# A linear-attention block and a token mixer on one core: five whole-operand weight sums move from VectorE to GpSimd

## The chip, the cores and the metric

The kernel runs on one core of a Trainium2 chip. The metric is the device time of one execution in microseconds (us). A core has a matrix engine (TensorE, "PE" in the profile, with its weight loads listed apart as "PEld"), VectorE ("DVE"), ScalarE ("ACT"), GpSimd ("POOL") and SyncE ("SP", which here only issues DMAs). Each engine works through its own queue in order, and they wait for one another by semaphores.

## The reference

The block has two halves with a residual each: linear attention with 32 heads over 2048 tokens of width 1024, then a mixer that multiplies along the token axis with a hidden width of 3584.

```python
def _B_ref(x, w1, b1, w2, b2):
    h = _layernorm(x, axis=-1)
    u = jnp.einsum("bsd,sf->bdf", h, w1) + b1
    u = _gelu(u)
    y = jnp.einsum("bdf,fs->bds", u, w2) + b2
    return (lambda x, *d: x.transpose(*d))(y, 0, 2, 1)

x = A_x
h = x + _A_ref(_layernorm(x, axis=-1), A_wqkv, A_wo)
h2 = h + _B_ref(_layernorm(h, axis=-1), B_w1, B_b1, B_w2, B_b2)
return h2
```

The change is in the first product of `_B_ref`, h (2048 x 1024, contracted over its 2048 tokens) with w1 (2048 x 3584).

## The kernel before

**Two levels of seven products.** Each of the mixer's two matrix products is made by a Strassen-Winograd scheme: a 2 x 2 block product from seven block products in place of eight, at the price of sums of operands beforehand and of results afterwards. The outer level splits tokens and columns in halves; for five of its seven products (1, 2, 3, 5 and 6) an inner level does the same again. Products 4 and 7 are made plainly.

**Names.** w1 is loaded in seven pieces, one for each `Quad` (a "pair of pairs": two `Mixer1`, each a pair of hidden blocks of 128). In its tile (`wq` in the profile) lie the four blocks a11, a12, a21 and a22 of 128 x 2048 elements. The outer scheme needs four sums of these, made for the whole Quad at once:

- sum 5 = a21 + a22, by a ScalarE cast (`cast5`) and an accumulating DMA (`add_a21`, line 164) issued by GpSimd;
- sum 7 = a21 - a11, in the same way (`cast7`, tile `sa7`);
- sum 6 = sum 5 - a11, one VectorE instruction of 128 x 2048 (`asums(6)`, tile `sa6`);
- sum 3 = a12 - sum 6, one VectorE instruction of 128 x 2048 (`asums(3)`, tile `sa3`).

All three `sa` tiles appear as "sa" in the profile, and there is one buffer of each. An inner scheme (`Inner`, `Inner2`) makes its own four small sums of an operand's quarters, "is" in the profile, 128 x 512 each, on VectorE: two when it is created (`sums(slice(0, 2))`), two more a little later (`rest`). It then runs i1, i5, i6, i2, i7, i3 and i4, four matmuls of 256 columns each, with additions into PSUM or SBUF tiles by VectorE and copies by ScalarE between them. The seven inner products each use one operand: a quarter of the outer operand (i1, i2, i4) or one of the "is" tiles (i5, i6, i7, i3).

**Order.** Quad 0 is done by `run_first`, Quad 1 by `run1`, and Quads 2 to 6 (`SIX = 2`) by `run1_six`, which the change touches. There the order of everything is written by hand. Five inner schemes follow each other: in1, in2, in6, in5, in3. `interleave` walks through each, putting matmuls of the plain products between (product 4 of the Quad before as `s4`, product 7 of this one as `s7`, 512 columns each), and at the named points "b", "c", "2", "7", "third" and "end" it calls what the dictionaries `at1`, `at2`, `at6`, `at5` and `at3` hold for them, in the order in which it was put there. The points of one inner scheme come in the order i1, "b", i5, i6, "c", i2, "2", i7, "7", i3, "third", i4, "end". On every engine the instructions stand in the order in which they are issued here.

In one Quad, sum 6 is made at "b" of in2; the second half of sum 7 (cast and GpSimd's DMA) at "2" of in2; sum 3 at "c" of in5; its first readers are the two first "is" of in3, made at "2" of in5, and then in3 itself. GpSimd's queue holds in this stretch only the accumulating DMAs: two for sum 7 of this Quad, then two for sum 5 of the next (at "7" of in5 and "c" of in3). SyncE's queue holds the loads of the next w1 piece, issued between in6 and in5.

`dve` is a wrapper of VectorE's instructions that keeps their program order; `pin` does that for a single instruction.

## Time and profile before

| | us |
|---|---|
| median of 3 runs | 547.6 (547.35 to 548.09) |
| the profiled execution | 547.9 |
| its span in the profile | 546.1 |
| time outside the span | 1.8 |
| attention half and start of the mixer, up to 262 us: TensorE busy | 260.15 |
| Quads 2 to 6, from sum 6 of the first, 272.79 to 384 (111.21 us): TensorE / VectorE / ScalarE / GpSimd busy | 111.21 / 102.40 / 77.39 / 23.11 |
| rest of the mixer, 384 to 546.1 (162.1 us): TensorE / VectorE busy | 158.54 / 141.37 |

The profile is that of one execution. Busy times are sums of instruction spans; the waits of an engine are attributed to what ended them. A line number is often that of a helper: L247 is the wrapper through which most instructions of VectorE, TensorE and ScalarE pass, so groups are told apart by their tiles, out<-in. The page's chain of waits, which follows the last instruction back to what released it, goes 88% over TensorE, 5% over DMAs, 3% over VectorE and 2% over ScalarE. Granted clock of TensorE is full throughout these stretches (1.00). All work of GpSimd in Quads 2 to 6 is 18 DMA issues, of 1.28 to 1.31 us each.

### The profile page before, as it was taken

How to read it: one execution, taken by the hardware profiler on the slowest of the kernel's cores; microseconds unless marked ns; L12 is line 12 of the kernel's file. 1: busy time of each engine (PE TensorE's matmuls, PEld its weight loads, DVE VectorE, ACT ScalarE, POOL GpSimd, SP SyncE). 2: the span in 40 equal slices, each digit the busy share in tenths (PEclk: the TensorE clock that was granted, in tenths of full speed). 3: DMA queues.
4: the chain of work that ended last, by engine and by line, in shares of the span. 5: the costliest groups of instructions: out<-in, count | busy, mean ns of one | idle time of the engine just before them, and what ended most of it. 6: DMA issues, size and time to landing. Idle time of an engine off the chain costs nothing.

```text
span 546.1 us, 10554 instructions
## 1 busy us (share of the span) xinstructions
PE 540.7 (99%) x4038; PEld 337.8 (62%) x4038; DVE 465.9 (85%) x926; ACT 312.7 (57%) x666; POOL 72.8 (13%) x78
## 2 busy tenths in 40 slices
PE   8999999999999999999999999999999999999997
PEld 3444446646864444456777777776455667877865
DVE  7798897867778577998999989989898899979777
ACT  5748677777687769667677677685220413313320
POOL 1000000000002350022023112220002103103111
PEclk9999999999999999999999999999999999999999
DMA  9933532200558999237365757756797749399343
GB/s 299 317 79 77 79 77 41 40 1 16 141 157 190 213 281 309 87 40 154 40 134 80 157 72 140 155 66 149 180 292 191 211 136 241 52 306 220 82 123 70
DMA packets 105378, 77.76 MB, mean 142 GB/s; under 512 B 16482, under 2 KB 97904, under 8 KB 105328
## 3 DMA queue, kind: packets, MB, share of 16 engines
q1 hardware_dynamic: 85536, 64.32, 42.3%
q0 software_dynamic: 19360, 12.34, 17.2%
q8 instruction: 31, 0.51, 0.4%
q10 hardware_dynamic: 432, 0.44, 0.3%
q14 instruction: 19, 0.16, 0.1%
HBM read 62.27 MB, written 11.67 MB: 135 GB/s over the span
## 4 chain that ended last, share of the span: by engine, by line
PE 88%; DMA 5%; DVE 3%; ACT 2%; issue 1%; POOL 0%; DVEq 0%; SPq 0%; POOLq 0%
PE psI L247 31%; PE psC L247 17%; PE psB L247 5%; PE psC L1198 4%; PE psB L1198 4%; PE psA L1198 4%; PE acc_t L1114 3%; PE psA L247 3%; DMA out_dram<-h_bf 2%; PE acc_t L247 2%; PE psE L1198 2%; PE psA L1332 2%; PE psC L1332 2%; PE psB L1332 2%; PE den_ps L247 1%
## 5 line engine op out<-in xcount | busy, mean ns | idle before, releaser
L247 PEld LDWEIGHTS <-is 128*128 128x128 f16 x900 | 88.0, 98 | 32.4 <-DVE is L247 0.2
L247 PEld LDWEIGHTS <-wq 128*128 128x128 bf16 (+1 forms) x694 | 67.9, 98 | 37.2 <-issue 0.7
L247 PE MATMUL acc_t<-wo_sb,pqT 128*128 128x512 f16 x256 | 55.9, 379 | 0.0
L247 PEld LDWEIGHTS <-sa 128*128 128x128 f16 x467 | 45.6, 98 | 13.9 <-issue 1.2
L247 PEld LDWEIGHTS <-pqT 128*128 128x128 bf16 x256 | 24.8, 98 | 30.5 <-issue 1.1
L520 POOL DMA_DIRECT2D out_dram<-wq x28 | 24.3, 936 | 143.5 <-ACT wq L523 120.4
L247 PE MATMUL psC<-gs,wq 128*128 128x512 f16 x168 | 40.8, 379 | 0.0
L1846 POOL DMA_DIRECT2D h_bf<-in_A_x_dram x18 | 15.8, 985 | 185.5 <-DMA wq<-in_B_w_dram 169.4
L247 PE MATMUL psI<-hi,is 128*128 128x256 f16 x240 | 36.0, 272 | 0.0
L247 PE MATMUL psC<-hT,wq 128*128 128x512 f16 x112 | 34.1, 379 | 0.0
L1198 PEld LDWEIGHTS <-xs 128*128 128x128 f16 x208 | 20.0, 98 | 22.2
L247 PE MATMUL psC<-hT,sa 128*128 128x512 f16 x112 | 32.0, 379 | 0.0
L247 ACT COPY psI<-psI 128x256 f32<-128x256 f32 x60 | 21.5, 358 | 16.1 <-PE psI L247 13.6
L247 PE MATMUL psI<-gi,is 128*128 128x256 f16 x210 | 27.8, 272 | 0.0
L164 POOL DMA_DIRECT2D wq<-in_B_w_dram x12 | 15.4, 1284 | 89.3 <-ACT wq L247 44.2
L1198 PE MATMUL psA<-wkv,xnT 128*128 128x512 bf16 x104 | 26.7, 379 | 0.0
L1198 PEld LDWEIGHTS <-xnT 128*128 128x128 bf16 x156 | 15.3, 98 | 17.9 <-issue 0.2
L247 DVE TENSOR_TENSOR t<-psI,t 128x256 f32<-128x256 f32 (+1 forms) x45 | 20.3, 473 | 6.3 <-PE psI L247 5.0
L201 DVE TENSOR_SCALAR e_sb<-e_sb 128x512 bf16<-128x512 bf16 x64 | 18.2, 284 | 6.5 <-ACT e_sb L196 6.4
L247 DVE TENSOR_TENSOR is<-wq 128x512 f16<-128x512 bf16 (+3 forms) x48 | 22.0, 458 | 0.0
L1114 PE MATMUL acc_t<-wkv,xnT 128*128 128x512 bf16 x96 | 21.7, 379 | 0.1
L1083 DVE BATCH_NORM_STATS2 st<-x_sb 128x6 f32<-128x512 bf16 x32 | 20.6, 681 | 0.9 <-DMA x_sb<-in_A_x_dram 0.9
(276 smaller groups left out, 1207.4 us busy)
## 6 DMA issues: line engine op xcount, KB each, us to landing
wq<-in_B_w_dram SPq DMA_DIRECT2D x20, 448.0 KB, 5.9
gs<-parked SPq DMA_DIRECT2D x9, 896.0 KB, 4.8
wq<-in_B_w_dram SPq DMA_DIRECT2D x11, 512.0 KB, 4.1
wq<-in_B_w_dram SPq DMA_DIRECT2D x5, 1024.0 KB, 7.1
shared_sb<-rd_dram SPq DMA_DIRECT2D x32, 128.0 KB, 5.3
out_dram<-h_bf SPq DMA_DIRECT2D x16, 256.0 KB, 4.5
x_sb<-in_A_x_dram SPq DMA_DIRECT2D x14, 256.0 KB, 3.9
w2o<-in_B_w_dram SPq DMA_DIRECT2D x4, 896.0 KB, 9.8
```

The source lines that it names most:

```text
L164: pin(nc.gpsimd.dma_start(t[:, ks, :], a21[:, ks, :], accum_op=ALU.add))
L201: pin(nc.vector.tensor_scalar(e_sb[:], e_sb[:], 1.0, PHI_EPS, ALU.min, ALU.add))
L247: return (lambda *a, **kw: pin(op(*a, **kw))) if self.always or getattr(Held, self.key) else op
L520: nc.gpsimd.dma_start(to, ot[:, a:b], accum_op=ALU.add)
L1083: return nc.vector.bn_stats(st[:, c, :], x_sb[:, c * CW:(c + 1) * CW])
L1114: mm = nc.tensor.matmul(pp[:, 0:CW], lhsT=xnT[:, kt, i * P:(i + 1) * P], rhs=wkv[:, kt, c * CW:(c + 1) * CW], start=(kt == 0), stop=(kt == ...
L1198: pin(nc.tensor.matmul(ps[:], lhsT=lhs[:, k, :], rhs=rhs[:, k, :], start=(start and k == 0), stop=(k == hk2 - 1), skip_group_check=True,))
L1332: pin(nc.tensor.matmul(out[:, j], lhsT=rhs[:, k, 2 * self.half + j, :], rhs=lhs[:, k], start=(start and j == 0 and k == 0), stop=(k == hk2 ...
L1846: pin(nc.gpsimd.dma_start(h_bfs[i][:, cols], x[rows(i), cols], accum_op=ALU.add))
```

## The change

`asums` gets an argument that sends its instruction to GpSimd. `run1_six` uses it for sum 3 and issues it at another point: at "third" of in2, behind what already stands there (the first GELU of this Quad on ScalarE), instead of at "c" of in5. The instruction reads the same blocks and writes the same tile; sums 5, 6 and 7 and the Quads 0 and 1 stay as they are.

```diff
-        def asums(self, m):
+        def asums(self, m, pool=False):
...
-            return dve.tensor_tensor(s5 if m == 5 else self.sa_tile(m), a, b, op)
+            return (pin(nc.gpsimd.tensor_tensor(self.sa_tile(m), a, b, op)) if pool else dve.tensor_tensor(s5 if m == 5 else self.sa_tile(m), a, b, op))
...
             put(at6, "third", make(5, Inner, self.mov5), lambda: sts[0].copy_c())
             put(at5, "b", rest(5))
             put(at5, "2", lambda: sts[1].copy_c())
-            put(at5, "c", step(self.asums, 3))
+            put(at2, "third", step(self.asums, 3, True))
             put(at5, "2", make(3, Inner2, self.mov3))
```

## The prediction

> **What bounds the kernel now.** I first read the page's busy times, to see which engine can set the end, then a table of windows over the stretch that the edit touches. The edit acts in the five pairs of pairs u = 2 to 6 of the first mixer. In the timeline of VectorE the sum of sub-matrix 6 ("sa<-wq", 128x2048) begins at 272.79, 295.01, 317.31, 339.54 and 361.77 us, once in each, so four whole periods can be cut out. These are the page's line and the windows (columns: span, busy time and count of each engine, granted clock, DMA share, GB/s):

> ```profile
> PE 540.7 (99%) x4038; PEld 337.8 (62%) x4038; DVE 465.9 (85%) x926; ACT 312.7 (57%) x666; POOL 72.8 (13%) x78
> ...
> 272.79:295.01 22.22, 22.22 (x174) 16.82 (x172) 20.42 (x48) 16.20 (x36) 5.13 (x4) 1.00 0.67 119
> 295.01:317.31 22.30, 22.30 (x175) 16.81 (x173) 20.54 (x49) 16.08 (x36) 5.17 (x4) 1.00 0.67 120
> 317.31:339.54 22.23, 22.23 (x175) 16.82 (x173) 20.44 (x49) 16.22 (x36) 5.13 (x4) 1.00 0.67 119
> 339.54:361.77 22.23, 22.23 (x175) 16.83 (x173) 20.44 (x49) 16.18 (x36) 5.13 (x4) 1.00 0.66 119
> ```

> A period is 22.245 us (361.77 - 272.79 = 88.98, by four). TensorE is busy for all of it, at full clock. Since its busy time is modelled, I check by starts: four 256-column matmuls take 0.435 us from start to start, two 512-column ones the same. A period holds 5 x 28 matmuls of the first kind (35 groups of four) and 32 of the second (16 pairs), so 51 x 0.435 = 22.19 us. Only some 0.06 us of a period is anything but matmuls at their pace. VectorE has 20.46 us of work in 22.245, so 1.8 us to spare, but all in small gaps: it works just ahead of TensorE.

> How little ahead is the second thing to see. This is VectorE and then TensorE in the second of these periods (timeline; columns: start us, length us, engine, line, operation, out<-in):

> ```profile
> 299.97 0.42 DVE L247 TENSOR_TENSOR e<-psI,t1a 128x256 f32<-128x256 f32 x1 [0.51 <-PE psI L247]
> 300.31 0.42 DVE L247 TENSOR_TENSOR is<-sa 128x512 f16<-128x512 f16 x1
> 300.64 0.42 DVE L247 TENSOR_TENSOR is<-sa,is 128x512 f16<-128x512 f16 x1
> 300.98 0.68 DVE L247 TENSOR_TENSOR t<-psI,t1a 128x512 f32<-128x512 f32 x1
> 301.86 0.43 DVE L247 TENSOR_TENSOR psB<-psI,t1a 128x256 f32<-128x256 f32 x1 [0.20 <-PE psI L247]
> 302.52 0.87 DVE L247 TENSOR_TENSOR psB<-psI,t 128x256 f32<-128x256 f32 x2 [0.22 <-PE psI L247]
> 303.29 0.42 DVE L247 TENSOR_TENSOR is<-wq 128x512 f16<-128x512 f16 x1
> ...
> 305.09 1.22 DVE L247 TENSOR_TENSOR sa<-wq,sa 128x2048 f16<-128x2048 bf16 x1
> 306.34 0.42 DVE L247 TENSOR_TENSOR is<-sa 128x512 f16<-128x512 f16 x1
> ```
> ```profile
> 302.31 0.60 PE L247 MATMUL psI<-hT,is 128*128 128x256 f16 x4
> ...
> 303.87 0.60 PE L247 MATMUL psI<-hE,is 128*128 128x256 f16 x4
> ...
> 308.22 0.60 PE L247 MATMUL psI<-hO,sa 128*128 128x256 f16 x4
> ```

> The weights "is" written at 303.29 (done 303.71) go into the matmuls of 303.87, whose weight load starts at 303.76: VectorE is 0.05 us early there. The one of 300.64 (done 301.06) is used at 302.31, with 1.2 us in hand. The whole-operand sum of 305.09 is read at 306.34 by VectorE and at 308.22 by TensorE, its weight load at 308.11.

> **What is removed.** Five VectorE instructions of 1.22 us (305.09 to the next start, 306.34: 1.25 us each). VectorE's work per period falls from 20.46 to 19.2 us. TensorE never waits for this sum, so the removal is worth at most the 0.06 us of a period that are not matmul pace: 5 x 0.06 = 0.3 us. That is the bound of any gain here.

> **What is added.** Five GpSimd sums of 128x2048, issued at "third" of in2. GpSimd's queue has two DMA issues of line 164 for this operand before it and those of the next operand behind it:

> ```profile
> 2.11 0.33 POOL masks.py:199 TENSOR_SCALAR_AFFINE_SELECT ident<-ident 128x128 bf16<-128x128 bf16 x1
> ...
> 299.05 1.29 POOL L164 DMA_DIRECT2D sa<-in_B_w_dram  x1 [1.55 <-ACT sa L247]
> 308.77 1.28 POOL L164 DMA_DIRECT2D wq<-in_B_w_dram  x1 [8.43 <-DVE e L247]
> ```

> Its operands are ready (sub-matrix 6 ends at 296.23) and the DMA issue ends at 300.34. At the start of the trace an elementwise instruction began 0.08 us after the DMA issue before it (2.03, then 2.11), so the sum starts at 300.42. The other four periods agree: the issues end at 278.10, 322.62, 344.85 and 367.08, each within 0.03 us of a VectorE "is<-sa" start. Until 308.77 the queue is empty, 8.43 us, so no DMA is delayed by a sum under that length.

> Its duration is shown by no row. On GpSimd a 128x1 fill takes 0.099 us, a 128x128 fill 0.204, the 128x128 select above 0.326. The fill's slope, (0.204 - 0.099)/127 = 0.83 ns an element, gives 1.8 us for 2048 and no input at all: the lower bound. The select, one input read and one output written, has (0.326 - 0.099)/127 = 1.79 ns, so 3.76 us; taken whole, sixteen times, it is 5.2, the upper bound. I take 3.76, the nearest row in kind. [...]

> **What it does to VectorE** is the large unknown: the trace has no GpSimd instruction that reads a tensor beside VectorE work. Descriptor work does not slow VectorE (the "is<-wq" of 318.44 keeps its 0.42 us inside the DMA issue of 318.19 to 319.47), but it reads no tensor. The bounds per period are nothing, and a VectorE that cannot start any instruction with two SBUF inputs until GpSimd is done. I take the second: here both engines stream whole operands out of the same memory, which no row shows them doing together for free, and VectorE's order leaves no room for even a short hold. [...]

> Worked out: GpSimd asks at 300.42, while the first "is<-sa" runs to 300.73, and then works to 300.73 + 3.76 = 304.49. The second "is" moves from 300.64 to 304.49. All that is behind it on VectorE, PSUM evacuations too, waits in order, although they read SBUF only once. From it to "is<-wq" are 0.34 + 0.60 + 0.33 + 0.77 = 2.04 us once the gaps for TensorE are squeezed out, so that one starts at 306.53 instead of 303.29: 3.24 late, less the 0.05 in hand, 3.2 us of TensorE standing still. Behind that VectorE gains 1.25 us from the missing sum, but TensorE, at its pace, cannot use it. GpSimd's sum is needed at 306.34 + 2 and is done long before. Each period repeats this: 5 x 3.2 = 16.0 us. The profiled execution took 547.9 with its span of 546.1, so it would be 563.9; the median is 0.3 below that one: **563.6 us**. With 1.8 us for the sum the loss is 1.25 a period (553.8), with 5.2 it is 4.6 (570.8).

> **Rivals.**
> - *VectorE keeps the memory through the pair, GpSimd comes in behind.* The two "is" run back to back, 0.33 us apart, and GpSimd may start only at 301.06. Then it overlaps just the PSUM evacuations until 303.29, and "is<-wq" waits to 304.82: 1.5 a period, 555.0 us (547.3 with a sum of 1.8 us, 562 with 5.2). For it: VectorE leaves no gap between the two; against: GpSimd has asked first.
> - *Both go on, slower.* Some five VectorE instructions of two SBUF inputs lie beside the sum; if each takes twice its 0.42, the two ahead of "is<-wq" cost nothing (1.2 in hand), that one 0.4 and the next as much: about 0.7 a period, 551 us.
> - *No interference: not slower.* Then the sum ends at 304.2 (at most 305.6), before 306.34; VectorE's reading "is<-sa" moves up to 305.09 and the relief is all there is: 547.6 - 0.3 = 547.3 us. It decides when VectorE's rows beside the sum keep 0.42 us and start on time. For it: from 300.98 to 303.29 VectorE mostly reads PSUM. Against: two "is" stand ahead of that stretch and one right behind.
> - *The sum comes late.* Above 7.7 us (300.42 to 308.11) TensorE waits for it directly; at 10 us, 5 x 2.3 = 11.5, 559 us. The upper bound of 5.2 speaks against it.

> **How the numbers follow.** The forecast 0.48, VectorE first 0.18, both slower 0.10, late sum 0.03: slower in 0.79 of cases. No interference 0.16, which lies within 0.2% (1.1 us, about what a measurement of this kernel tells from no change). Faster by more than that would need TensorE not to be the limit in these periods; 0.05 for that. The range 547.2 to 568.5 takes in the rivals and the forecast up to a sum of 4.7 us; the rest of its tail, and a gain, are left out. The forecast's own range is 553.8 to 570.8.

> **What would show it.** Right: five GpSimd rows of 3 to 5 us; an idle VectorE (or a stretched "is") right behind the first "is<-sa", TensorE gaps near 3 us a period, waiting for "is", and periods of 25.4 us between two "sa<-wq". VectorE first: the gap sits ahead of "is<-wq" instead. Wrong altogether: periods still 22.2 us. A duration other than 3.76 moves the time by 5 us for each 1 us.

## The result and the profile after

The changed kernel takes 571.45 us (median of 4 runs, 569.88 to 572.04) against 547.48 us before (547.24 to 548.09): a ratio of 1.043 with a 95% interval of 1.0416 to 1.0443, 24.0 us slower. The profiled execution took 571.49, its span is 569.7 us; that is 23.6 more than the span before.

First the page of the changed kernel: busy times of the engines, then the group of GpSimd's new instructions and that of the small sums made from "sa" (columns: group and count, busy us, mean ns, idle time ahead).

```profile
PE 548.6 (96%) x4022; PEld 340.8 (60%) x4038; DVE 479.2 (84%) x921; ACT 312.8 (55%) x666; POOL 93.3 (16%) x83
...
L247 DVE TENSOR_TENSOR is<-sa 128x512 f16<-128x512 f16 (+1 forms) x36 | 37.7, 1047 | 0.0
...
L635 POOL TENSOR_TENSOR sa<-wq,sa 128x2048 f16<-128x2048 bf16 x5 | 22.9, 4590 | 0.0
```

VectorE lost five instructions of 1.22 us and is yet 13.3 us busier: an instruction that is held counts as busy. The 36 "is<-sa" of all shapes took 17.8 us before (9.2 + 8.6 in the two groups by shape) and take 37.7 now. GpSimd's sum takes 4.59 us.

The same four periods as before, from one sum 6 to the next (windows: span, busy time and count of PE, PEld, DVE, ACT, POOL, then granted clock):

```profile
272.20:299.23 27.03, 24.06 (x175) 17.45 (x173) 23.22 (x47) 16.28 (x36) 9.23 (x5) 0.94 0.55 98
299.23:326.37 27.14, 24.07 (x174) 17.43 (x172) 23.17 (x47) 16.12 (x35) 9.26 (x5) 0.94 0.55 98
326.37:353.60 27.23, 24.17 (x175) 17.39 (x173) 23.17 (x48) 16.14 (x35) 9.22 (x5) 0.94 0.54 97
353.60:380.85 27.25, 24.19 (x174) 17.48 (x172) 23.14 (x47) 16.12 (x35) 9.22 (x5) 0.94 0.54 97
```

(The first row begins 0.06 us ahead of its sum 6, which starts at 272.26.) The mean from there is 27.15 us in place of 22.245: 4.90 a period. TensorE, all of the period before, is now busy for 24.1, and its clock, 1.00 before, is 0.94 on average. So two things were lost in a period: some 3 us of standstill, and something by the clock. The timeline of the second period shows both, GpSimd and VectorE first, then TensorE:

```profile
303.27 1.29 POOL L164 DMA_DIRECT2D sa<-in_B_w_dram  x1 [1.60 <-DVE e L247]
304.04 4.60 POOL L635 TENSOR_TENSOR sa<-wq,sa 128x2048 f16<-128x2048 bf16 x1
304.19 0.42 DVE L247 TENSOR_TENSOR e<-psI,t1a 128x256 f32<-128x256 f32 x1 [0.51 <-PE psI L247]
304.53 4.41 DVE L247 TENSOR_TENSOR is<-sa 128x512 f16<-128x512 f16 x1
308.86 0.41 DVE L247 TENSOR_TENSOR is<-sa,is 128x512 f16<-128x512 f16 x1
...
310.79 0.41 DVE L247 TENSOR_TENSOR is<-wq 128x512 f16<-128x512 f16 x1
```
```profile
305.88 0.38 PE L247 MATMUL psC<-hT,wq 128*128 128x512 f16 x1
308.99 0.61 PE L247 MATMUL psI<-hi,is 128*128 128x256 f16 x4 [2.73 <-DVE is L247]
...
309.88 0.38 PE L247 MATMUL psC<-hT,wq 128*128 128x512 f16 x1
310.59 1.01 PE L247 MATMUL psI<-hi,sa 128*128 128x256 f16 x4 [0.34 <-DVE psB L247]
311.40 1.06 PE L247 MATMUL psI<-hE,wq 128*128 128x256 f16 x4
312.25 1.06 PE L247 MATMUL psI<-hE,is 128*128 128x256 f16 x4
```

GpSimd's sum runs from 304.04 to 308.64. The evacuation of 304.19, which reads PSUM and one SBUF operand, keeps its 0.42 us beside it. The small sum of 304.53 reads two SBUF operands and takes 4.41 instead of 0.42: it ends 0.30 us behind GpSimd. TensorE waits 2.73 us for it, at the product i7 of in6, and another 0.34 for an evacuation. Then the four-matmul groups, 0.435 us from start to start before, follow each other after 0.81 and 0.85. That is the clock (windows as above, over single microseconds):

```profile
309.00:310.00 1.00, 1.00 (x9) 0.89 (x10) 1.00 (x3) 0.00 (x0) 0.00 (x0) 1.00 0.00 0
310.00:311.00 1.00, 0.66 (x5) 0.28 (x3) 1.00 (x4) 0.04 (x1) 0.00 (x0) 0.68 0.00 0
311.00:312.00 1.00, 1.00 (x6) 0.73 (x5) 0.96 (x4) 0.53 (x1) 0.00 (x0) 0.50 0.20 41
312.00:313.00 1.00, 1.00 (x7) 0.71 (x5) 1.00 (x4) 0.50 (x2) 0.00 (x0) 0.50 0.97 280
313.00:314.00 1.00, 1.00 (x6) 0.46 (x5) 0.49 (x2) 0.72 (x2) 0.00 (x0) 0.62 1.17 334
```

What is missing from 1.00 adds up to 0.32 + 0.50 + 0.50 + 0.38 = 1.70 us: a stretch of 3.4 us at half clock, here from 310.35 to 313.77, and one like it in each of the five periods. TensorE's waits over all of them (who waited for whom, us in total, times, longest) are:

```profile
PE psI L247 <- DVE is L247: 13.6, 5, 2.7
PE psI L247 <- DVE psB L247: 1.6, 5, 0.3
```

These waits, 13.6 + 1.6 = 15.2 us, are counted from the modelled end of the matmul before, and are less than what TensorE loses. By starts (a 512-column matmul takes 0.22 us from start to start), the first wait puts it back by 308.99 - 305.88 - 0.22 = 2.89 us and the second by 310.59 - 309.88 - 0.22 = 0.49. That is 3.38 a period, 16.9 in five. Of the 4.90 us of a period 1.52 are left for the clock, 7.6 in five. This is less than 5 x 1.70 = 8.5, since part of a slow stretch can fall into a wait (310.35 to 310.59 here). Together 24.5 us, against 24.0 between the medians and 23.6 between the two profiled spans (the changed one reaches its first sum 6 already 0.5 us sooner).

### The profile page after: what moved, and what is told of

It is laid out like the page before. It is cut to its first block, busy times and chain, and to the rows that moved or that the text cites. A ratio compares the mean times of both kernels' runs of the same rounds, so it can differ in the third digit from the quotient of the medians.

```text
span 569.7 us, 10549 instructions
## 1 busy us (share of the span) xinstructions
PE 548.6 (96%) x4022; PEld 340.8 (60%) x4038; DVE 479.2 (84%) x921; ACT 312.8 (55%) x666; POOL 93.3 (16%) x83
## 4 chain that ended last, share of the span: by engine, by line
PE 93%; DVE 6%; issue 1%; ACT 0%; DVEq 0%
PE psI L247 29%; PE psC L247 17%; PE acc_t L247 10%; PE psB L247 5%; DVE is L247 4%; PE psC L1198 4%; PE psB L1198 4%; PE psA L1198 4%; PE psA L247 3%; PE acc_t L1114 3%; PE psE L1198 2%; PE psA L1332 2%; PE psC L1332 2%; PE psB L1332 2%; PE den_ps L247 1%; PE acc_t L1549 1%
## 5 line engine op out<-in xcount | busy, mean ns | idle before, releaser
L247 PEld LDWEIGHTS <-is 128*128 128x128 f16 x900 | 88.9, 99 | 49.5 <-DVE is L247 16.9
L247 PEld LDWEIGHTS <-wq 128*128 128x128 bf16 (+1 forms) x694 | 68.9, 99 | 37.7
L247 PEld LDWEIGHTS <-sa 128*128 128x128 f16 x467 | 46.7, 100 | 17.2 <-issue 3.3
L247 PE MATMUL acc_t<-wo_sb,pqT 128*128 128x512 f16 x256 | 55.9, 379 | 0.0
L247 PE MATMUL psI<-hi,is 128*128 128x256 f16 x240 | 36.2, 273 | 13.6 <-DVE is L247 13.6
L247 PEld LDWEIGHTS <-pqT 128*128 128x128 bf16 x256 | 24.8, 98 | 30.6 <-issue 1.1
L247 PE MATMUL psC<-gs,wq 128*128 128x512 f16 x168 | 40.8, 379 | 0.0
L247 DVE TENSOR_TENSOR is<-sa 128x512 f16<-128x512 f16 (+1 forms) x36 | 37.7, 1047 | 0.0
L247 ACT COPY psI<-psI 128x256 f32<-128x256 f32 x60 | 21.5, 358 | 25.1 <-PE psI L247 22.8
L247 PE MATMUL psC<-hT,wq 128*128 128x512 f16 x112 | 34.2, 380 | 0.0
L247 PE MATMUL psC<-hT,sa 128*128 128x512 f16 x112 | 33.9, 397 | 0.0
L1198 PEld LDWEIGHTS <-xs 128*128 128x128 f16 x208 | 20.0, 98 | 22.2
L164 POOL DMA_DIRECT2D wq<-in_B_w_dram x12 | 15.5, 1290 | 92.2 <-ACT wq L247 80.6
L247 PE MATMUL psI<-gi,is 128*128 128x256 f16 x210 | 27.8, 273 | 0.0
L247 DVE TENSOR_TENSOR t<-psI,t 128x256 f32<-128x256 f32 (+1 forms) x45 | 20.7, 474 | 7.5 <-PE psI L247 6.3
L635 POOL TENSOR_TENSOR sa<-wq,sa 128x2048 f16<-128x2048 bf16 x5 | 22.9, 4590 | 0.0
L164 POOL DMA_DIRECT2D sa<-in_B_w_dram x12 | 15.4, 1307 | 42.7 <-ACT sa L247 23.4
```

The lines of the kernel that those rows point to most:

```text
L164: pin(nc.gpsimd.dma_start(t[:, ks, :], a21[:, ks, :], accum_op=ALU.add))
L247: return (lambda *a, **kw: pin(op(*a, **kw))) if self.always or getattr(Held, self.key) else op
L635: return (pin(nc.gpsimd.tensor_tensor(self.sa_tile(m), a, b, op)) if pool else dve.tensor_tensor(s5 if m == 5 else self.sa_tile(m), a, b, op))
L1198: pin(nc.tensor.matmul(ps[:], lhsT=lhs[:, k, :], rhs=rhs[:, k, :], start=(start and k == 0), stop=(k == hk2 - 1), skip_group_check=True,))
```

## The experiments

Theory H: GpSimd's sum holds VectorE's instructions with two SBUF inputs until it ends, TensorE stands still for that, and the standstill halves its clock for 3.4 us. "Before" beside each group of runs was 547.5 to 547.7 us. All edits are to the changed kernel. `part3(engine, ks)` stands for sum 3 over the pieces `ks` of 256 elements, on the engine named.

### Place or engine?

Two runs take the change apart: the new place alone, and the new engine alone.

```diff
-            put(at2, "third", step(self.asums, 3, True))
+            put(at2, "third", step(self.asums, 3))
```

> Sum 3 is issued at the new point, "third" of in2, but on VectorE. Theory H (GpSimd's sum holds VectorE's two-input instructions until it ends, TensorE stands still for it, and its clock is halved afterwards): the move alone costs what VectorE loses there, 1.22 us less its gap of 0.51 before the evacuation at 299.97 and of 0.42 behind, some 0.3 us a period, 547.5 to 549.5 us, clock 1.00 throughout. Rival R2 (the earlier point itself disturbs the order of the work, whichever engine does it): most of the loss appears here too, 560 us or more.

548.21 us, ratio 1.0012 (1.0002 to 1.0021), clock 1.00. The periods are 22.35 us (sum 6 at 272.74 and, four later, at 362.13), 0.1 longer, where some 0.3 was expected; R2 falls.

```diff
-            put(at2, "third", step(self.asums, 3, True))
+            put(at5, "c", step(self.asums, 3, True))
```

> Sum 3 is made by GpSimd, but issued at the old point, "c" of in5. Theory H: GpSimd's queue holds nothing between the two points and its operands are ready at both, so the sum starts at the same moment as in the changed kernel: 571 us, 27.1 us a period. Rival R2 (the point matters): the sum starts some 4 us later in the period and the loss differs by more than 3 us from that of the changed kernel.

571.35 us, ratio 1.0433 (1.0416 to 1.0451), the time of the changed kernel. The engine is the cause; with nothing else in GpSimd's queue between the two places, the place in the program decided nothing. GpSimd's sum starts 4.81 us after VectorE's sum 6 in both kernels (299.83 to 304.64 here, 299.23 to 304.04 in the changed kernel):

```profile
304.64 4.60 POOL L635 TENSOR_TENSOR sa<-wq,sa 128x2048 f16<-128x2048 bf16 x1
```

### Where do the slow matmuls come from?

The hold without GpSimd: VectorE repeats sum 3 three times ahead of the pair of small sums. The copies write the same values.

```diff
-            put(at2, "third", step(self.asums, 3, True))
-            put(at6, "b", self.base3, rest(6))
+            put(at6, "b", self.base3, *[step(self.part3, nc.vector, slice(0, 8))] * 3, rest(6))
```

> No GpSimd sum at all: VectorE makes sum 3 three times over, one after the other, right ahead of the pair of small sums in in6 (point "b"), 3 x 1.14 to 1.22 = 3.5 us in which it does nothing else. Theory H: TensorE stands still for some 2.4 us at the product i7 of in6 and loses 3.1 us a period by VectorE's lateness, and the granted clock falls to a half for a stretch of 3.4 us behind it, another 1.5 a period: 570 us with five such stretches, fewer where the standstill is too short. Rival R1 (the slow matmuls come from GpSimd reading the memory, not from the standstill): clock 1.00, 563 us.

567.27 us, ratio 1.0363 (1.0342 to 1.0384), mean clock 0.987. The clock fell without any GpSimd sum, so R1 falls. In the profiled execution it fell in four of the five periods: sum 6 starts at 272.68, 299.06, 325.62, 352.54 and 377.81, and the period from 352.54, which keeps 1.00, has 25.27 us where the three before it have 26.4 to 26.9. The matmuls wait 2.40 us in each of the five, then slow down in four:

```profile
308.49 0.61 PE L247 MATMUL psI<-hi,is 128*128 128x256 f16 x4 [2.40 <-DVE is L247]
...
310.09 1.01 PE L247 MATMUL psI<-hi,sa 128*128 128x256 f16 x4
310.90 1.06 PE L247 MATMUL psI<-hE,wq 128*128 128x256 f16 x4
```

The same with two copies in place of three:

> As with three sums on VectorE ahead of the pair, but two: the pair comes 1.14 us earlier. Theory H: a standstill of some 1.2 us a period in place of 2.4, a loss of 1.9 a period, and no stretch at half clock, since the standstill is too short: 557 us, clock 1.00. Rival R9 (any standstill of TensorE lowers the clock): stretches at a half appear, 560 us or more.

556.33 us, ratio 1.0151 (1.0134 to 1.0168), clock 1.00, periods of 24.01 us. TensorE waits 1.14 us, and nothing slows down. R9 falls: a standstill of 1.14 us costs only itself (by starts 1.30 us, and 0.50 at the evacuation behind it; a period is 1.77 longer).

```profile
305.23 0.61 PE L247 MATMUL psI<-hi,is 128*128 128x256 f16 x4 [1.14 <-DVE is L247]
```

The other way round: GpSimd's sum and the hold stay, but TensorE is kept busy in the meantime, with zero weights added to a PSUM tile.

```diff
+            def keep_busy(n=25):
+                for i in range(n):
+                    pe.matmul(self.in6.c, lhsT=zero[:], rhs=self.in6.mov[7][:, i % 4, :], start=False, stop=False, skip_group_check=True)
...
             put(at6, "b", self.base3, rest(6))
+            put(at6, "2", keep_busy)
...
+    zero = pools["t"].tile([P, P], FP16, tag="zero", name="zero")
+    dve.memset(zero[:], 0.0)
```

> The changed kernel with 25 more matmuls of 256 columns in each period, zero weights added into the PSUM tile of in6 at its point "2", so that TensorE is busy (25 x 0.109 = 2.7 us) while it would stand still. Theory H: VectorE is held as before, but the clock stays at 1.00; the loss of 4.85 a period shrinks by the 1.5 of the slow stretch to 3.3: 564 us. Rival R1 (the slow stretch comes from GpSimd): 571 us or more, with the clock at a half as in the changed kernel.

564.12 us, ratio 1.0304 (1.0288 to 1.032): 7.3 us faster than the changed kernel, with 125 matmuls more. The small sum is still held, for 4.41 us, but the matmuls behind keep their pace of 0.435 us:

```profile
303.57 4.41 DVE L247 TENSOR_TENSOR is<-sa 128x512 f16<-128x512 f16 x1
...
305.09 2.89 PE L247 MATMUL psI<-hi,zero 128*128 128x256 f16 x25
...
309.63 0.60 PE L247 MATMUL psI<-hi,sa 128*128 128x256 f16 x4 [0.34 <-DVE psB L247]
310.07 0.60 PE L247 MATMUL psI<-hE,wq 128*128 128x256 f16 x4
310.50 0.60 PE L247 MATMUL psI<-hE,is 128*128 128x256 f16 x4
```

So the loss splits into the hold, 564.1 - 547.5 = 16.6 us, and the clock, 571.4 - 564.1 = 7.3 us (by the starts above, 16.9 and 7.6).

The traces also show behind which waits the clock falls. Within a run, all its changes lie at whole multiples of 3.413 us from one another: in the changed kernel it falls at 283.05, 310.35, 337.66, 364.97 and 392.27 (27.31, that is 8 x 3.413, apart), and it rises 3.41 us after each. Cut at these marks, the 13 traces of this case have some 2060 windows of 3.413 us. A fall stands behind each of the 15 windows in which TensorE was idle for 2.08 to 2.73 us, and behind none of the others at full clock, in which it was idle for 1.76 us at most. With three copies, 2.14 to 2.40 us of idle time lie in one window in the four periods in which the clock falls. In the remaining one, the fourth, the mark at 360.54 cuts the wait of 2.40 us into 0.98 and 1.42; with 0.34 for the evacuation the second window has 1.76, and the clock stays. Here are a window of each kind and the one behind it (columns: window, length, PE busy, ..., with the granted clock third from the end; the idle time is length less PE busy):

```profile
305.93:309.34 3.41, 1.01 (x9) 0.77 (x9) 3.38 (x6) 0.00 (x0) 0.00 (x0) 1.00 0.45 55
309.34:312.76 3.42, 3.36 (x16) 2.04 (x15) 3.35 (x11) 1.33 (x3) 0.00 (x0) 0.50 0.37 99
...
360.54:363.96 3.42, 1.66 (x13) 1.25 (x14) 3.42 (x8) 0.03 (x1) 0.00 (x0) 1.00 0.02 2
363.96:367.37 3.41, 3.41 (x28) 2.58 (x27) 2.45 (x8) 2.98 (x7) 0.00 (x0) 1.00 0.83 229
```

So in these traces the length of the wait alone doesn't decide, but how much of it falls into one window.

### What holds VectorE?

Half of the sum on GpSimd, half on VectorE:

```diff
-            put(at2, "third", step(self.asums, 3, True))
+            put(at2, "third", step(self.part3, nc.gpsimd, slice(0, 4)))
+            put(at5, "c", step(self.part3, nc.vector, slice(4, 8)))
```

> GpSimd makes only the first half of sum 3 (128x1024) at the new point, VectorE the other half at the old one. Theory H: a sum of about 2.35 us by the changed kernel's 4.59 for twice the elements, so VectorE's first small sum ends some 2.2 us earlier than in the changed kernel; the loss falls from 3.35 to about 1.2 us a period, the standstill is too short for the clock to fall: 553.5 us, clock 1.00. Rival R3 (the hold does not go by the sum's length): VectorE's first small sum is still stretched to over 4 us and the time stays above 560 us.

554.12 us, ratio 1.0128 (1.0111 to 1.0145), clock 1.00. The hold goes by the length of GpSimd's sum: 2.67 us of it stretch the small sum to 2.47. R3 falls.

```profile
300.83 2.67 POOL L641 TENSOR_TENSOR sa<-wq,sa 128x1024 f16<-128x1024 bf16 x1
...
301.32 2.47 DVE L247 TENSOR_TENSOR is<-sa 128x512 f16<-128x512 f16 x1
```

Then two GpSimd instructions that the result does not need, into the tile of sum 3, which VectorE fills afterwards as before the change: one that only writes, and one with a single input.

```diff
+        def fill3(self):
+            pin(nc.gpsimd.memset(self.sa_tile(3), 0.0))
...
-            put(at2, "third", step(self.asums, 3, True))
+            put(at2, "third", self.fill3)
+            put(at5, "c", step(self.part3, nc.vector, slice(0, 8)))
```

> GpSimd fills the tile of sum 3 with zeros (128x2048, no input) at the new point, and VectorE makes sum 3 into it at the old point as before. By the fill of 128x128 in the profile it takes some 1.8 us, over the pair of small sums. Theory H, in the form that it is GpSimd's reading that holds VectorE: small sums keep 0.42 us, 547.5 us. Rival R4 (any elementwise work of GpSimd holds VectorE): the first small sum is stretched to about 1.6 us, a loss of 0.8 a period, 551.5 us.

547.76 us, ratio 1.0000 (0.9990 to 1.0010). The fill of 2.36 us lies over the pair of small sums, and they keep 0.41 and 0.42 us; R4 falls:

```profile
301.43 2.36 POOL L644 MEMSET sa<- 128x2048 f16 x1
...
301.94 0.41 DVE L247 TENSOR_TENSOR is<-sa 128x512 f16<-128x512 f16 x1
302.27 0.42 DVE L247 TENSOR_TENSOR is<-sa,is 128x512 f16<-128x512 f16 x1
```

```diff
+        def copy3(self):
+            pin(nc.gpsimd.tensor_copy(self.sa_tile(3), self.S[6]))
...
-            put(at2, "third", step(self.asums, 3, True))
+            put(at2, "third", self.copy3)
+            put(at5, "c", step(self.part3, nc.vector, slice(0, 8)))
```

> GpSimd copies sum 6 into the tile of sum 3 (128x2048, one input) at the new point, and VectorE makes sum 3 into it at the old point as before. Theory H (reading holds, with one input too): VectorE's first small sum is stretched to the end of the copy, whatever that is; with 3.8 us, by the select's row, the loss is 2.5 a period, 560 us, with 1.8 us 0.8 a period, 551.5 us. Rival R5 (only a GpSimd instruction of two inputs holds): 0.42 us, 547.5 us.

553.12 us, ratio 1.0107 (1.0092 to 1.0122), clock 1.00. The copy, as long as the fill but reading, does hold: R5 falls.

```profile
300.46 2.44 POOL L644 COPY sa<-sa 128x2048 f16<-128x2048 f16 x1
...
300.97 2.22 DVE L247 TENSOR_TENSOR is<-sa 128x512 f16<-128x512 f16 x1
```

Which of VectorE's instructions are held is seen when the whole sum starts behind the pair. VectorE writes one column of the tile there, and GpSimd has to wait for that.

```diff
+        def gate3(self):
+            pin(nc.vector.memset(self.sa_tile(3)[:, 0, 0:1], 0.0))
...
-            put(at2, "third", step(self.asums, 3, True))
-            put(at6, "b", self.base3, rest(6))
+            put(at6, "b", self.base3, rest(6), self.gate3, step(self.part3, nc.gpsimd, slice(0, 8)))
```

> GpSimd's whole sum starts only after the pair of small sums in in6: VectorE writes one column of the tile of sum 3 behind the pair, and GpSimd has to wait for that. Theory H: the sum lies from 301.2 to 305.8 in the second period of before; the PSUM evacuations beside it, which read SBUF once, keep their 0.4 to 0.7 us, and the small sum of 303.29 waits to 305.8: 2.5 us a period, at i5 of in5 instead of i7 of in6; 560 us with the clock at 1.00, up to 567.5 if it falls in each period. Rival R6 (all VectorE work is held, PSUM evacuations too): they are stretched, and the loss is as large as in the changed kernel or larger, 571 us.

556.15 us, ratio 1.0161 (1.0146 to 1.0176), clock 1.00. The evacuations beside the sum keep 0.43 us each; the next small sum is stretched to 2.36 and TensorE waits for it, 1.68 us, at i5 of in5. R6 falls. This small sum reads sum 5, in the block a21, and GpSimd reads a12 and sum 6: the hold doesn't need common operands. The loss is 8.5 us, less than the 12.5 forecast, in the main since the sum takes 4.05 us here and not 4.59 (2.7 of the 4.0 us).

```profile
302.57 4.05 POOL L641 TENSOR_TENSOR sa<-wq,sa 128x2048 f16<-128x2048 bf16 x1 [0.98 <-DVE sa L644]
303.10 0.43 DVE L247 TENSOR_TENSOR psB<-psI,t1a 128x256 f32<-128x256 f32 x1 [0.19 <-PE psI L247]
303.76 0.87 DVE L247 TENSOR_TENSOR psB<-psI,t 128x256 f32<-128x256 f32 x2 [0.22 <-PE psI L247]
304.54 2.36 DVE L247 TENSOR_TENSOR is<-wq 128x512 f16<-128x512 f16 x1
```

### Can GpSimd help at all here?

The sum at its new place, but in eight instructions:

```diff
-            put(at2, "third", step(self.asums, 3, True))
+            for k in range(8):
+                put(at2, "third", step(self.part3, nc.gpsimd, slice(k, k + 1)))
```

> GpSimd's sum in eight instructions of 128x256 at the new point, the same elements in all. By 4.05 us for 2048 and 2.66 - 0.52 = 2.14 for 1024 elements a piece takes some 0.7 us, together 5.6. Theory H, with the access handed over between instructions: each of VectorE's two-input instructions waits for the rest of one piece, no row of it is longer than about 1.2 us, some 1 us a period is lost and the clock stays at 1.00: 550 to 555 us. Rival R7 (GpSimd keeps the access as long as its queue has work): one small sum is stretched to over 4.5 us, 571 us or more.

555.27 us, ratio 1.0133 (1.0117 to 1.015). The time is as expected, but not for the reason given. Sum 6 starts at 272.86, 295.38, 317.91, 346.69 and 369.22: three periods of 22.53 us, 0.28 longer than before, and one of 28.78. In the short ones VectorE gets in between the pieces; in the long one it doesn't, and GpSimd keeps it out for all eight. Here are two of them, the first short, the second long:

```profile
300.20 6.81 POOL L641 TENSOR_TENSOR sa<-wq,sa 128x256 f16<-128x256 bf16 x8
...
300.68 0.50 DVE L247 TENSOR_TENSOR is<-sa 128x512 f16<-128x512 f16 x1
301.11 0.89 DVE L247 TENSOR_TENSOR is<-sa,is 128x512 f16<-128x512 f16 x1
```
```profile
322.72 5.54 POOL L641 TENSOR_TENSOR sa<-wq,sa 128x256 f16<-128x256 bf16 x8
...
323.21 5.35 DVE L247 TENSOR_TENSOR is<-sa 128x512 f16<-128x512 f16 x1
```

So VectorE gets in as H has it in four periods, and is kept out as R7 has it in one; what decides between them stays open. In the long period the clock, expected at 1.00, falls too: TensorE waits 3.67 us, and the clock is at a half from 327.41 to 334.24, two windows of 3.41, in the first of which TensorE still stands idle for 1.20. Of the four executions one took 565.34 us, the others 555.1 to 555.3; that one has no profile.

Last, half the sum, started behind the pair, so that it fits into the stretch in which VectorE reads PSUM:

```diff
-            put(at2, "third", step(self.asums, 3, True))
-            put(at6, "b", self.base3, rest(6))
+            put(at6, "b", self.base3, rest(6), self.gate3, step(self.part3, nc.gpsimd, slice(0, 4)))
+            put(at5, "c", step(self.part3, nc.vector, slice(4, 8)))
```

> GpSimd makes half of sum 3 (128x1024), started behind the pair of small sums in in6, VectorE the other half at the old point. Theory H: some 2.1 us of GpSimd lie in the stretch of 2.4 us in which VectorE reads PSUM only; the small sum behind it is held by at most 0.2 us, and VectorE's relief of half a sum cannot be used: 547.4 to 548.7 us. Rival R8 (the bound on the gain is wrong and VectorE's relief does shorten the periods): below 546.4 us, periods under 22.0 us.

547.33 us, ratio 0.9994 (0.9984 to 1.0004). GpSimd's 2.12 us, from 301.19 to 303.31 in the profile, end 0.15 us behind the start of the next small sum at 303.16, which takes 0.43 us. Periods are 22.23 us. The hold is gone, and so is any effect: VectorE's relief of half a sum gains nothing that can be told from no change, as the bound on the gain said; R8 falls.

```profile
301.19 2.12 POOL L641 TENSOR_TENSOR sa<-wq,sa 128x1024 f16<-128x1024 bf16 x1 [0.98 <-DVE sa L644]
...
303.16 0.43 DVE L247 TENSOR_TENSOR is<-wq 128x512 f16<-128x512 f16 x1
```

## Why the prediction was wrong, point by point

- **TensorE is the limit, a gain at most 0.3 us:** right. With half the sum on GpSimd and no hold, the periods stay at 22.23 us.
- **VectorE held until GpSimd is done:** right, chosen from between two bounds without a row of this kernel for it. The runs show it: instructions with two SBUF inputs are held (0.42 becomes 4.41 us), evacuations from PSUM are not (0.42, 0.43); a GpSimd copy of 2.44 us holds (2.22 for the small sum beside it), a fill of 2.36 does not (0.41). That GpSimd in its turn waits for a small sum already running, as the forecast had it from 300.42 to 300.73, no run shows: in all five periods GpSimd's sum started first, 0.49 us ahead of the small sum. The nearest to it are the eight pieces, 6.81 us in the short period shown, where VectorE's small sums came in between, and 5.54 in the long one.
- **Start of the sum:** wrong. It was put at the end of the DMA issue, from one row at the start of the trace, and would have caught the second small sum of the pair. It starts 0.77 us after the issue's start, 0.52 before its end, and catches the first.
- **Length of the sum:** 3.76 us forecast, 4.59 measured, 4.05 where it does not start beside a DMA issue. By luck, start and length nearly cancel: the sum ends 4.11 us after the start of the first small sum (308.64 - 304.53); forecast were 4.18 (304.49 - 300.31).
- **TensorE's standstill:** "is<-wq" was forecast 3.24 us late. Before, it follows the first small sum of the pair by 2.98 us (303.29 - 300.31), now by 6.26 (310.79 - 304.53): 3.28. But TensorE does not wait where the forecast had it wait, at the matmuls of "is<-wq": it stands still at i7 of in6, four products earlier, for the first small sum of the pair, and then for an evacuation. By starts the standstills come to 16.9 us, forecast 16.0. The run with the matmuls that keep TensorE busy, where only this loss is left, takes 564.12 us; the forecast was 563.6. That they agree so well owes something to the two errors above that cancel.
- **What failed is the sum's assumption that TensorE stands still and then goes on at its pace.** The term for the granted clock is missing altogether. The windows of before have 1.00 in each, and no TensorE wait in those periods to learn from; the question of what a standstill of 3 us does to the clock was not put. It halves it for 3.4 us, which costs 1.52 us a period, 7.6 by the trace and 7.3 by the run with TensorE kept busy. With it, 563.6 becomes 570.9 to 571.2. That the upper end of the range, 568.5, was drawn by the sum's length alone (4.7 us) is the same omission. The clock fell without TensorE being idle for the whole of a window of 3.413 us: 2.08 us of it were enough, 1.76 were not.
- **A hint was there.** The kernel before opens with matmuls of zeros whose result it doesn't use, from a function called `warm_up`, and its trace shows six of them, of 512 columns, 0.43 us apart, where later ones are 0.22 apart. That is the same half pace, behind 1.20 us in which TensorE had nothing to do. The windows don't show it, since the trace has no record of the clock before 6.97 us and the column then reads 1.00.

```profile
1.20 2.74 PE L104 MATMUL acc_t<-warm 128*128 128x512 bf16 x6 [1.20 <-DVE m L112]
...
16.28 5.34 PE L1114 MATMUL acc_t<-wkv,xnT 128*128 128x512 bf16 x24
```

## What to carry to other kernels

In the runs here, work on GpSimd that read SBUF did not run beside VectorE's sums of two SBUF inputs (0.42 us became 2.22 to 4.41 beside one GpSimd instruction of 2.44 to 4.60): look which such sums fall into its time, how far ahead of TensorE they run, and put it only where VectorE reads PSUM (0.42 to 0.43 us for an evacuation beside such a sum). Where TensorE is the limit, as here, relief of another engine has no value to weigh against that (ratio 0.9994 with half the sum moved and no hold). And price a standstill that leaves TensorE idle for 2.08 us or more of one window of 3.413 us twice, once as the wait and once as the slow stretch behind it, 1.5 us here.
